# New written instruction orders for all five engines of a chunked-attention and attention-experts kernel

## The chip, the core and the metric

The kernel runs on one core of one Trainium2 chip. The metric is the device time of one execution in microseconds. The median of three runs of the kernel before is 377.94 us (377.81 to 377.98).

## What is computed

Eight batches of 576 rows. First an attention with 8 heads of 64 columns in which each chunk of 64 rows looks only at itself; its output, 512 columns wide, is the input x of a layer with four experts. Each expert is a causal attention over all 576 rows with a projection out; a softmax over the two largest gate logits of a row weighs the experts.

```python
scores = scale * np.matmul(q_c, k_c.transpose(0, 1, 2, 4, 3))     # per chunk of 64 rows
attn = np.exp(scores - max);  attn = attn / (sum + 1e-09)
x = np.matmul(attn, v_c)                                          # -> (B, S, H * D)
logits = x @ w_gate;  w = softmax over the 2 largest of 4
for e in range(E):
    q, k, v = x @ wq[e], x @ wk[e], x @ wv[e]
    a = softmax(where(causal, -1e9, scale * (q @ k.T)))
    out += mask_e * w_e * (a @ v @ wo[e])
```

## The kernel before

The kernel does not issue its instructions in the order in which its code runs. It builds a plan: `add` makes an `Op` for an engine with a closure that issues its instructions, the ops that it depends on, and the buffers it uses (2457 ops, the DMAs among them). `Plan.emit` then plays the plan on a clock of its own and calls the closures in turn. Each engine takes its ops strictly in the rank that the table `ORDER` (line 191) gives: a list of numbers for each of PE, DVE, ACT, Pool (GpSimd) and SP, where the number is the place of the op among the ops of its engine. The tables fix the order on each engine, and through the clock also which of the interchangeable buffers (8 banks of PSUM, 4 `at`, 2 `aT` and so on) an op gets. While the planner's clock is below `WARM` = 25 us and PE has nothing ready, it issues a warm-up matmul (line 847, 128x512 bf16, result not used).

The steps on PE, by the line of their matmuls:

- L471: scores of the chunked attention, quarters of the array (64x64), 32 matmuls for a group of 128 rows; most steps take two groups. L544: the same attention times v, also quarters, 32 matmuls a group. 36 groups in all.
- L369: transposes, 8 matmuls for a normalised tile `en` (first five groups), 14 for the weights `at` of one expert and batch.
- L589: projections of x to q and k, 12 matmuls of 256 or 320 columns in three passes (high and low parts). L443: v and the gate, 12 matmuls of 260 columns ("V"). L810: output projection, 6 matmuls of 512 columns ("output"). These use the full array.
- L686: expert scores, 6 or 12 matmuls with 64 rows of the array ("rows" form, as L369). L780: weights times v, 4 and 20 matmuls with 64 columns of the array ("cols" form).

`scores` (L686) needs two `at` buffers for its two experts and keeps them until their transposes are done. For a step of 128 or 256 columns, VectorE takes the minimum (L697), ScalarE the exponential (L709) and GpSimd the product with the gate (L731); L755 on ScalarE clears the banks that the transposes filled. In the chunked attention, L481 to L490 on VectorE, L486 on ScalarE and L499 on GpSimd (`en`) stand between L471 and the transposes; from the sixth group on the transposes are DMAs (L376, L385). The weights come in by DMA, and L415 (ScalarE) and L419 (VectorE or GpSimd) split them into high and low parts (`wvg_lo`, `wqk_lo`, `wo_lo`).

```python
for eng, text in ORDER.items():
    own = [o for o in self.ops if o.eng == eng]
    for r, k in enumerate(text.split()):
        own[int(k)].rank = r
...
    if got is None:
        if eng == "PE" and now < until:
            fill()
```

Of the kernel before, what the change touches and what calls it, by code (L numbers as in the profile page):

```python
# [186 lines left out]
def pool_t(n):  # L187
# [15 lines left out]
    """,  # L203
    "DVE": """
# [20 lines left out]
    """,  # L225
    "ACT": """
# [23 lines left out]
    """,  # L250
    "Pool": """
# [635 lines left out]
```

## Time and profile before

| | |
|---|---|
| median of 3 runs | 377.94 us |
| the profiled execution: device time | 378.73 us |
| its span, first to last instruction | 377.0 us |
| granted TensorE clock, mean | 0.998 |
| PE busy | 369.2 us, 98% of the span |
| weight loads (PEld) busy | 315.9 us |
| ScalarE, VectorE, GpSimd busy | 302.5, 265.9, 244.9 us |
| DMA | 57.25 MB, 152 GB/s |

The profile tells for each engine when an instruction started and how long it took, and for each hole which semaphore ended it. Matmuls are pipelined, and their ends are modelled: how long a step holds PE is read from the start of its first matmul to the start of the next step's. A matmul and its weight load are two instructions; the profile lists the loads as an engine of their own, PEld.

### The profile page before, as it was taken

The page shows a single profiled execution, that of the slowest core. Times are in us where ns is not written, and L with a number is a line of the kernel's source. Part 1 is how long each engine was busy: PE and PEld are TensorE (multiplying, and loading weights), DVE is VectorE, ACT ScalarE, POOL GpSimd, SP SyncE. Part 2 cuts the span into 40 slices and gives each one's busy share as a digit, 9 for nine tenths or more (in the row PEclk, how much of TensorE's full clock was granted, in tenths as well). Part 3 has the DMA queues.
Part 4 walks back from the last instruction along what each step waited for, and adds up shares of the span by engine and source line. Part 5 has one row for each costly group of instructions (what it writes and reads, how often), then busy time and mean ns, then how long its engine had stood idle before and what let it go on. Part 6 is the DMA issues. An engine that isn't in the chain of part 4 may idle for free.

```text
span 377.0 us, 13434 instructions
## 1 busy us (share of the span) xinstructions
PE 369.2 (98%) x5214; PEld 315.9 (84%) x5217; DVE 265.9 (71%) x895; ACT 302.5 (80%) x845; POOL 244.9 (65%) x447
## 2 busy tenths in 40 slices
PE   8999999999999999999999989999999999999996
PEld 3699889988889799887899789978898989976775
DVE  2778899679967953589697786867864675388631
ACT  2574799999987996898966889699985895799651
POOL 6481778996899059966774518998684039867700
PEclk9999999999999999999999999999999999999999
DMA  7968679579888703249799395669526002235634
GB/s 286 386 226 269 162 190 252 83 180 164 196 199 194 145 30 85 56 114 253 192 251 233 58 238 137 101 173 155 153 62 113 2 3 57 57 57 93 178 123 167
DMA packets 88624, 57.25 MB, mean 152 GB/s; under 512 B 68976, under 2 KB 69232, under 8 KB 88560
## 3 DMA queue, kind: packets, MB, share of 16 engines
q1 hardware_dynamic: 88416, 56.12, 59.0%
q8 instruction: 41, 0.67, 0.7%
q10 hardware_dynamic: 144, 0.26, 0.2%
q14 instruction: 23, 0.19, 0.2%
HBM read 30.42 MB, written 9.44 MB: 106 GB/s over the span
## 4 chain that ended last, share of the span: by engine, by line
PE 73%; ACT 10%; DMA 5%; DVE 4%; POOL 4%; issue 2%; SPq 1%; POOLq 0%; ACTq 0%; DVEq 0%
PE bank L589 19%; PE bank L810 14%; PE bank L443 11%; PE bank L780 11%; PE bank L686 8%; ACT at L709 5%; PE bank L544 4%; PE bank L369 4%; PE bank L471 3%; DMA wpT<-wp 2%; DMA vs<-in_vt_dram 1%; POOL at L731 1%; ACT et L385 1%; DMA qs<-in_qt_dram 1%; ACT e L486 1%
## 5 line engine op out<-in xcount | busy, mean ns | idle before, releaser
L731 POOL TENSOR_SCALAR at<-at,st,gate 128x192 f32<-128x192 f32 (+4 forms) x160 | 94.8, 604 | 12.2 <-DVE st L722 4.5
L709 ACT ACTIVATE at<-at,st 128x576 f32<-128x576 f32 (+4 forms) x160 | 89.7, 584 | 4.0 <-DVE st L697 3.8
L589 PE MATMUL bank<-xh,wqk_hi 128*128 128x256 f32 (+1 forms) x256 | 77.3, 302 | 0.0
L589 PE MATMUL bank<-xl,wqk_hi 128*128 128x256 f32 (+1 forms) x256 | 75.7, 296 | 0.0
L589 PE MATMUL bank<-xh,wqk_lo 128*128 128x256 f32 (+1 forms) x256 | 75.7, 296 | 0.0
L697 DVE CUSTOM_DVE_ANT_0 at<-bank,mask 128x320 f32<-128x320 f32 (+4 forms) x160 | 59.9, 421 | 13.7 <-PE bank L686 11.7
L499 POOL TENSOR_TENSOR en<-e,mx 128x512 f32<-128x512 f32 x36 | 37.5, 1054 | 29.1 <-DVE mx L490 25.1
L589 PEld LDWEIGHTS bank<-xh,wqk_hi 128*128 128x128 f32 x256 | 48.4, 189 | 2.3 <-issue 0.5
L589 PEld LDWEIGHTS bank<-xl,wqk_hi 128*128 128x128 f32 x256 | 48.5, 189 | 0.2
L589 PEld LDWEIGHTS bank<-xh,wqk_lo 128*128 128x128 f32 x256 | 48.5, 189 | 0.0
L780 PE MATMUL bank<-aT,vv 128*64 128x448 f32 (+4 forms) x384 | 46.9, 393 | 0.0
L780 PEld LDWEIGHTS bank<-aT,vv 128*64 128x64 f32 x384 | 24.6, 137 | 22.2 <-issue 15.5
L763 DVE STREAM_TRANSPOSE aT<-at 32x96 f32<-32x96 f32 x128 | 34.4, 269 | 11.8 <-PE bank L780 6.3
L385 ACT ACTIVATE et<-wpT 128x1024 uint16<-128x1024 uint16 x31 | 36.7, 1189 | 5.7 <-DMA wpT<-wp 5.4
L755 ACT ACTIVATE aT<-bank 128x128 f32<-128x128 f32 (+1 forms) x160 | 37.0, 338 | 3.3 <-PE bank L369 3.2
L385 ACT ACTIVATE aT<-wpT 128x1024 uint16<-128x1024 uint16 x32 | 38.2, 1199 | 1.0 <-DMA wpT<-wp 0.9
L443 PE MATMUL bank<-wvg_hi,xh 128*128 128x260 f32 x128 | 36.8, 288 | 0.0
L443 PE MATMUL bank<-wvg_lo,xh 128*128 128x260 f32 x128 | 36.2, 283 | 0.0
L443 PE MATMUL bank<-wvg_hi,xl 128*128 128x260 f32 x128 | 36.0, 281 | 0.0
L709 ACT ACTIVATION_READ_ACCUMULATOR at<-at,st 128x1 f32 (+1 forms) x160 | 35.4, 221 | 0.0
L376 POOL COPY wp<-at 128x1024 uint16<-128x1024 uint16 x32 | 32.6, 1034 | 0.2
L686 PE MATMUL bank<-kh,qh 64*128 64x288 f32 (+4 forms) x192 | 32.5, 325 | 0.2
(104 smaller groups left out, 896.8 us busy)
## 6 DMA issues: line engine op xcount, KB each, us to landing
ks<-in_kt_dram SPq DMA_DIRECT2D x36, 256.0 KB, 4.1
vs<-in_vt_dram SPq DMA_DIRECT2D x36, 256.0 KB, 4.4
qs<-in_qt_dram SPq DMA_DIRECT2D x35, 256.0 KB, 4.4
out_dram<-y SPq DMA_DIRECT2D x35, 256.0 KB, 2.1
at<-in_wqk_dram SPq DMA_DIRECT2D x4, 256.0 KB, 5.9
wpT<-wp SPq DMA_TRANSPOSE x63, 3.3
at<-in_wvg_dram SPq DMA_DIRECT2D x2, 260.0 KB, 4.8
at<-in_wo_dram SPq DMA_DIRECT2D x2, 256.0 KB, 6.5
```

Source lines behind the costliest of these rows:

```text
L385: act.activation(put().bitcast(U16).rearrange("p j (q x) -> p j q x", x=2), pt.t[:, :256 * n].rearrange("p (x j q) -> p j q x", x=2, j=n), ...
L443: pe.matmul(bk.t[0:rows, :W_VG], xp[:, k, cols], wp[:, k, :], start=(n == 0), stop=(n == 3 * KT - 1))
L499: pool.tensor_tensor(en.t.rearrange("p (s h k) -> p s h k", s=2, h=HP), ev, rv.to_broadcast([128, 2, HP, 64]), op=OP.mult)
L589: pe.matmul(bk.t[:, :c1 - c0], wp[:, k], xp[:, k, c0:c1], start=(n == 0), stop=(n == 3 * KT - 1))
L686: pe.matmul(bks[s].t[:rows(i), at:at + c1 - c0], q[own, cs], k[own, c0:c1], start=(x == 0), stop=(x == 2), skip_group_check=True)
L697: dve.tensor_tensor_reduce(out=a.t[:r, A_OFF[i] + c0:A_OFF[i] + c1], in0=bk.t[:r, at:at + w], in1=mask[:r, m0:m0 + w], scale=1.0, scalar=f ...
L709: act.activation(af, af, AF.Exp, scale=-1.0, bias=st.t[:r, 0, i, 0:1], accum_out=st.t[:r, 1, i, 0:1])
L731: pool.tensor_scalar(af, af, st.t[:r, 2, i, 0:1], gt.t[:r, i, e:e + 1], op0=OP.mult, op1=OP.mult)
L755: act.activation(dst, bk.t[:, s0:s0 + 64 * n].rearrange("p (j c) -> p j c", j=n), AF.Copy)
L763: dve.transpose(dst, src)
L780: pe.matmul(bk.t[64 * s:64 * s + 64, c0 - h0:h1 - h0], vs.t[:, j, 64 * (2 * pair + s):64 * (2 * pair + s) + 64], ts[s].t[:, 448 * j + c0:4 ...
L810: pe.matmul(bk.t[:, n0:n1], up[:, k, 128 * t:128 * t + 128], wp[:, k, n0:n1], start=(n == 0), stop=(n == 5), skip_group_check=True)
```

## The change

All five tables of `ORDER` are replaced. Nothing else is touched: the ops, their closures, buffers, costs and the planner are the same. Of the diff (the first lines of two tables; the other rows are numbers too):

```diff
 ORDER = {
     "PE": """
-3 0 9 4 1 6 2 5 57 61 12 10 7 55 63 53 13 8 11 16 14 58 64 18 60 62 59 73 15 75 76 20 74 56 54 17 68 66 67 65 90 24
+0 3 6 9 1 4 2 5 12 7 10 63 11 58 55 53 13 8 16 61 14 57 18 62 56 54 64 65 20 60 75 74 67 59 15 24 17 68 73 66 76 93
...
     "SP": """
-10 4 8 12 14 11 5 9 13 1 15 2 16 0 3 24 7 6 18 20 17 37 26 21 31 36 19 38 32 30 23 22 42 47 28 29 27 25 34 35 59 45
+8 4 10 9 12 14 0 1 15 3 11 5 16 13 2 24 7 6 20 18 17 37 26 21 31 38 36 19 30 32 22 23 42 47 28 29 59 27 25 45 35 33
```

PE holds 314 steps in both orders. Warm-up matmuls that the planner puts between them: 43 before, 51 now (10 and 5 ahead of the second step in both; then 17, 2, 2 and 7 before, and 15, 7, 4 and 10 now).

**The fifth batch's first groups on PE.** Before, in PE's row (L544 and L471 are the quarter steps; a row with another `et`, `vs`, `ks` or `qs` is another group):

```order
L544 MATMUL bank_65<-et_86,vs_80 64x64 x2
...
L544 MATMUL bank_65<-et_85,vs_77 64x64 x2
...
L544 MATMUL bank_63<-et_88,vs_78 64x64 x2
...
L544 MATMUL bank_63<-et_87,vs_79 64x64 x2
...
L471 MATMUL bank_68<-ks_75,qs_71 64x64 x2
...
L471 MATMUL bank_68<-ks_76,qs_72 64x64 x2
...
L686 MATMUL bank_62<-kh_102,qh_98 128x192
...
L471 MATMUL bank_61<-ks_73,qs_69 64x64 x2
...
L443 MATMUL bank_63<-wvg_hi,xch_89 128x260
```

The same groups' steps now:

```order
L544 MATMUL bank_61<-et_87,vs_80 64x64 x2
...
L544 MATMUL bank_61<-et_86,vs_78 64x64 x2
...
L471 MATMUL bank_68<-ks_73,qs_69 64x64 x2
...
L471 MATMUL bank_68<-ks_76,qs_72 64x64 x2
...
L810 MATMUL bank_62<-wo_hi,uh 128x512
...
L443 MATMUL bank_63<-wvg_hi,xch_89 128x260
...
L810 MATMUL bank_65<-wo_hi,uh 128x512
...
L471 MATMUL bank_64<-ks_74,qs_70 64x64 x2
...
L544 MATMUL bank_66<-et_85,vs_79 64x64 x2
...
L544 MATMUL bank_66<-et_88,vs_77 64x64 x2
...
L810 MATMUL bank_61<-wo_hi,uh 128x512
```

Seven groups' quarter work stood in one stretch with one score step in it; now four groups' stand together, then an output, a V and an output step, then three groups', then an output step.

**GpSimd while the weights come in.** Before, in GpSimd's row (`en` is the normalised tile of a group, which an L369 step on PE waits for):

```order
L499 TENSOR_TENSOR en_83<-e_81,mx_93 128x512
L499 TENSOR_TENSOR en_84<-e_82,mx_94 128x512
L419 TENSOR_TENSOR wqk_lo<-at_109,wqk_hi 128x512
L419 TENSOR_TENSOR wo_lo<-at_110,wo_hi 128x512
L499 TENSOR_TENSOR en_83<-e_81,mx_91 128x512
L419 TENSOR_TENSOR wo_lo<-at_110,wo_hi 128x512
L499 TENSOR_TENSOR en_84<-e_82,mx_92 128x512
```

Now:

```order
L499 TENSOR_TENSOR en_83<-e_81,mx_93 128x512
L419 TENSOR_TENSOR wqk_lo<-at_109,wqk_hi 128x512
L499 TENSOR_TENSOR en_84<-e_82,mx_94 128x512
L419 TENSOR_TENSOR wvg_lo<-at_107,wvg_hi 128x520
L499 TENSOR_TENSOR en_83<-e_81,mx_91 128x512
L419 TENSOR_TENSOR wo_lo<-at_110,wo_hi 128x512 x2
L499 TENSOR_TENSOR en_84<-e_82,mx_92 128x512
```

The fifth group's `en` (from `e_81`, `mx_91`) stood behind the first half of `wo_lo`; now it stands ahead of both halves, behind the second half of `wvg_lo`.

**The last batch's transposes on PE.** Before, two transposes of two experts' weights in a row, then the output step:

```order
L369 MATMUL bank_62<-ident,at_109 128x64 x2
L369 MATMUL bank_67<-ident,at_109 128x64 x2
...
L369 MATMUL bank_61<-ident,at_110 128x64 x2
L369 MATMUL bank_66<-ident,at_110 128x64 x2
...
L810 MATMUL bank_67<-wo_hi,uh 128x512
```

Now:

```order
L369 MATMUL bank_68<-ident,at_110 128x64 x2
L369 MATMUL bank_64<-ident,at_110 128x64 x2
...
L810 MATMUL bank_61<-wo_hi,uh 128x512
...
L369 MATMUL bank_63<-ident,at_109 128x64 x2
L369 MATMUL bank_64<-ident,at_109 128x64 x2
...
L810 MATMUL bank_68<-wo_hi,uh 128x512
```

An output step has come between the two, and the step behind them writes a bank that the first transpose filled.

## Rows read from the trace of the kernel before

**Rows 1.** The page's first part: busy time, share of the span and instructions of each engine.

```profile
PE 369.2 (98%) x5214; PEld 315.9 (84%) x5217; DVE 265.9 (71%) x895; ACT 302.5 (80%) x845; POOL 244.9 (65%) x447
```

**Rows 2.** The page's second part: TensorE's granted clock in 40 equal slices of the span, in tenths.

```profile
PEclk9999999999999999999999999999999999999999
```

**Rows 3.** The page's fourth part: the chain that ended last, its share of the span by engine.

```profile
PE 73%; ACT 10%; DMA 5%; DVE 4%; POOL 4%; issue 2%; SPq 1%; POOLq 0%; ACTq 0%; DVEq 0%
```

**Rows 4.** The waits of PE's matmuls over the whole span: who waited for whom, us in total, times, longest.

```profile
PE bank L471 <- issue: 1.3, 1, 1.3
...
PE bank L810 <- ACT aT L755: 0.6, 1, 0.6
```

**Rows 5.** PE in order of time from 216 to 223 us: start, length, instruction, count, and in brackets the idle time ahead of it and what ended it.

```profile
216.17 2.10 PE L544 MATMUL bank<-et,vs 64*64 64x64 f32 x128
218.09 1.11 PE L471 MATMUL bank<-ks,qs 64*64 64x64 f32 x64
...
220.11 0.33 PE L471 MATMUL bank<-ks,qs 64*64 64x64 f32 x2
221.76 0.69 PE L471 MATMUL bank<-ks,qs 64*64 64x64 f32 x30 [1.33 <-issue]
222.38 0.39 PE L443 MATMUL bank<-wvg_hi,xch 128*128 128x260 f32 x1
```

**Rows 6.** PE in order of time near the program's start, columns as in rows 5 (the profile has lost the record of one of the 17 warm-up matmuls from 8.63 us).

```profile
8.63 3.84 PE L847 MATMUL bank<-warm 128*128 128x512 bf16 x16
12.40 0.69 PE L471 MATMUL bank<-ks,qs 64*64 64x64 f32 x32
13.03 0.46 PE L369 MATMUL bank<-ident,en 64*128 64x64 f32 x8
...
17.95 0.47 PE L443 MATMUL bank<-wvg_hi,xh 128*128 128x260 f32 x1
```

**Rows 7.** The page's third part: one of the DMA queues, its packets, MB, and share of 16 engines' span.

```profile
q8 instruction: 41, 0.67, 0.7%
```

**Rows 8.** The DMA queues from 219.0 to 220.4 us alone, columns as in rows 7.

```profile
q1 hardware_dynamic: 226, 0.41, 83.4%
q8 instruction: 1, 0.02, 4.2%
```

**Rows 9.** Pieces of the chain that ended last, in order of time: start, length, engine and line, matmuls. Each is a whole step or a run of equal steps.

```profile
161.49 1.03 PE bank L369 x28
...
173.23 0.58 PE bank L369 x14
...
183.18 1.09 PE bank L471 x64
...
191.70 1.39 PE bank L810 x6
...
194.53 2.02 PE bank L471 x128
...
208.67 0.84 PE bank L686 x12
...
232.99 1.43 PE bank L589 x12
```

**Rows 10.** PE in order of time in two dense stretches, from 27 and from 192.9 us, columns as in rows 5.

```profile
27.24 0.46 PE L369 MATMUL bank<-ident,en 64*128 64x64 f32 x8 [0.30 <-POOL en L499]
27.63 1.16 PE L544 MATMUL bank<-et,vs 64*64 64x64 f32 x64
28.61 1.11 PE L471 MATMUL bank<-ks,qs 64*64 64x64 f32 x64
29.55 0.65 PE L544 MATMUL bank<-et,vs 64*64 64x64 f32 x32
...
192.93 0.28 PE L443 MATMUL bank<-wvg_hi,xh 128*128 128x260 f32 x1
...
194.46 2.10 PE L471 MATMUL bank<-ks,qs 64*64 64x64 f32 x128
196.48 0.39 PE L589 MATMUL bank<-xh,wqk_hi 128*128 128x256 f32 x1
...
198.02 0.31 PE L589 MATMUL bank<-xh,wqk_hi 128*128 128x320 f32 x1
```

**Rows 11.** GpSimd in order of time from 24 us, columns as in rows 5.

```profile
24.88 1.30 POOL L419 TENSOR_TENSOR wo_lo<-at,wo_hi 128x512 fp32r<-128x512 f32 x1 [1.52 <-ACT wo_hi L415]
26.15 1.04 POOL L499 TENSOR_TENSOR en<-e,mx 128x512 f32<-128x512 f32 x1
```

**Rows 12.** PE in order of time: the first row of a step and of the step behind it, at three places, columns as in rows 5.

```profile
86.05 1.61 PE L544 MATMUL bank<-et,vs 64*64 64x64 f32 x64
87.59 0.40 PE L686 MATMUL bank<-kh,qh 64*128 64x288 f32 x2
...
120.90 0.75 PE L686 MATMUL bank<-kh,qh 64*128 64x192 f32 x2
...
122.25 1.19 PE L544 MATMUL bank<-et,vs 64*64 64x64 f32 x64
...
344.74 1.10 PE L369 MATMUL bank<-ident,at 64*128 64x64 f32 x28
346.45 0.50 PE L810 MATMUL bank<-wo_hi,uh 128*128 128x512 f32 x1 [0.61 <-ACT aT L755]
```

134 rows, old and new, of the table ORDER are left out of this document.

## The prediction

> **What bounds the kernel now.** The page's first part comes first: TensorE is busy for 369.2 of 377.0 us, the next engine, ScalarE, for 302.5 [rows 1]. A busy PE need not be PE at its best, so the slices come next: its clock is granted in full in all forty [rows 2], and the time is not lost there. The chain that ended last runs over PE for 73% of the span [rows 3]. So what counts is how the steps on PE follow each other, and the wait view filtered to PE names the two largest holes behind the first microseconds: 1.3 us once at L471 for "issue", and 0.6 us at L810 for ScalarE [rows 4]. "Issue" means that PE waited for nothing that the profile shows: no semaphore ended that wait.
>
> PE in order of time shows the place. From 216.17 us it runs 128 quarter matmuls of L544, 64 of L471, 12 score matmuls and 2 of the next L471 step, then stands still until 221.76 [rows 5] (the score step's place is told in the order). The whole L471 step of one group lasts from 220.11 to 222.38, 2.27 us; the same step between other steps lasts from 12.40 to 13.03, 0.63 us [rows 6]. **The pause costs 1.64 us.**
>
> What came late? PE's matmuls and weight loads are 10,431 instructions [rows 1]; one DMA queue of kind "instruction" moved 41 packets, 0.67 MB [rows 7], one for every 254 of them. One of these packets lies inside 219.0 to 220.4 us, the stretch just ahead of the pause, in which the data queue took 83.4% of the DMA engines [rows 8]. I read the pause as PE waiting for its next block of instructions. From 216.17 to 220.11 it had run 204 matmuls, each with its own weight load: 408 instructions in 3.94 us, more than one packet holds. Where full steps run, one matmul and its load go every 0.12 us, so a packet feeds 15 us; a quarter step of 64 matmuls uses 128 instructions in about 1 us.
>
> [...]
>
> **Term 1: the pause goes, -1.64 us.** In the new order the five groups' steps that stood as L544, L544, L471, scores, L471 stand as L544, L471 (256 instructions), then output, V and output, then L471 and L544 (192 instructions). The three full steps between are 24 matmuls and last over 4 us at the rows of such steps (1.43 for twelve V or projection matmuls, 1.39 for an output step [rows 9]). From the stretch in which the late packet moved (219.0 to 220.4 [rows 8]) to the moment PE went on (221.76) it is under 2.8 us, so 4 us should be enough. Dense stretches remain elsewhere: the densest in the new order is L544, L544, L471 for five groups, 160 matmuls or 320 instructions in a row, and a pair of two-group L544 steps, 256, in two places. For these the rows speak: 168 matmuls from 27.24 to 30.20 us (29.55 + 0.65), 336 instructions in 2.96 us, ran with no hole behind the first wait, and 256 instructions from 194.46 to 196.48 ran with none either [rows 10]. So I take no new pause; the other end is one more of the same size.
>
> **Term 2: eight more warm-up matmuls, +1.78 us.** The planner fills PE's empty time up to 25 us of its own clock with L847 matmuls. The old order held 43, the new one 51. They are in PE's program and run even when the next step is ready. Seventeen of them last from 8.63 to 12.40 us, 0.222 each [rows 6]; eight cost 1.78. In front of the last of them both orders have done the same real work (four L471 steps, two transposes, two L544 steps), so all 306 steps that remain start that much later. Against this nothing can hide: PE has no idle time behind it into which 1.78 us would fit, except the waits of term 4. The lower end is 0, if in the old order the last matmuls had been waiting for data and the new order starts with data ready.
>
> **Term 3: changes of form, +0.57 us.** PE's steps have four forms (full, quarters, rows, cols), and a step costs more beside another form. A pair of two-group L471 steps lasts 2.02, one alone 1.09: a run of quarters costs 2 x 1.09 - 2.02 = 0.16. Two transposes together last 1.03, one alone 0.58: a run of rows costs 0.13 [rows 9]. A V step before quarters lasts from 192.93 to 194.46, 1.53, and a 256-column projection behind them from 196.48 to 198.02, 1.54 [rows 10], where twelve matmuls between full steps take 1.43 [rows 9]: a run of full steps costs 0.10 + 0.11, some 0.20. After the warm-up both orders have 306 steps and 16 runs of cols; full runs go from 32 to 36, quarter runs from 23 to 24, rows runs from 34 to 31. That is 4 x 0.20 + 0.16 - 3 x 0.13 = +0.57. Bounds: 0.13 to 0.20 for each of the two more runs, 0.3 to 0.8.
>
> **Term 4: other waits, -0.98 us.** Four are worth naming. (a) At 27.24 us the L369 step waits 0.30 us for the GpSimd product en [rows 10], which GpSimd began at 26.15, behind 1.30 us of wo_lo [rows 11]. In the new order this product stands ahead of both wo_lo pieces on GpSimd: gone. (b) At 344.74 two transposes last until the output step at 346.45, 1.71 us where a pair takes 1.03 [rows 9, 12]: 0.68 us, of which the profile shows 0.61 as PE waiting for ScalarE to clear the bank (aT, L755). In the new order an output step stands between the two transposes and gives ScalarE 1.4 us: gone. (c) The L544 step at 86.05 lasts until the score step at 87.59, 1.54 us, where a quarter step alone takes 1.09 [rows 9, 12]: 0.45. (d) Twelve score matmuls last from 120.90 to 122.25, 1.35 us, where twelve take 0.84 [rows 9, 12]; less 0.10 for the change of form (above, 0.16 to 0.20 for the two changes of a run), 0.41 is a wait. For these two I see no reason in the order that they go, nor that they grow, since every engine's order is new; I take them unchanged (0.86 us), with 0 and double as the ends.
>
> **What is moved beside PE.** All lists are new, so DMA issues on SP and the waits behind them shift too. Where GpSimd, VectorE and ScalarE are earlier or later by some us the time does not change as long as PE finds its inputs: they are busy 64 to 80% [rows 1]. The tail behind the last matmul is the same halves of the last output step, and I cost it at nothing.
>
> **Sum.** -1.64 + 1.78 + 0.57 - 0.98 = -0.27 us. The profiled execution took 378.73 us, its span 377.0 and 1.7 around it; it lies 0.8 above the median of the three runs, 377.94, and I carry the difference over to the median: **377.7 us**, no change that can be told (0.2% is 0.76 us, about what a measurement of this kernel can tell from none).
>
> **Rivals.**
> 1. *The pause moves instead of going* (slower). For it: the rows show that density alone does not decide, since 336 instructions in 2.96 us ran through and 408 in 3.94 us did not; where a packet ends and how busy the DMA engines are (83% ahead of the pause) must count too. The new order keeps 320 instructions in a row at one place, and a two-group pair right behind score steps and ahead of a values step. It decides once a packet's worth is used up before the next has come, some 4 us after the last. Against: only one of 41 did so before. Price: one pause, 377.7 + 1.64 = 379.3.
> 2. *The change doesn't do what it says.* If code is always in time, the pause belongs to something else in that stretch (the loads that began at 218 us, say) and stays: also 377.7 + 1.64 = 379.3. The packet in that stretch and the lack of any releaser speak against it.
> 3. *The waits shrink more than I take.* An order written anew may serve all four: -1.84 instead of -0.98, so 377.7 - 0.86 = 376.8, and 376.5 with term 3 at its lower end. For it: two of four go visibly. Against: score steps still follow score steps, and they need a new weight buffer each time.
> 4. *A new wait of that kind* of 0.5 to 1.3 us: 378.2 to 379.0.
>
> **How the numbers follow.** Forecast 0.46; rival 1 0.18, rival 2 0.05, rival 3 0.26, rival 4 0.05. The forecast's own spread (terms 2 and 3 down to their lower ends against the two waits doubled) leaves it mostly within 0.2%. Rival 3 makes the chance of faster 0.27 with a little of the forecast's lower side, rivals 1, 2 and 4 that of slower 0.27; the rest, 0.46, is no change. The range reaches from rival 3's lower time to rivals 1 and 2: 376.5 to 379.3.
>
> **What would show it.** Right: no "issue" wait of over 0.5 us on PE behind the warm-up; 51 warm-up matmuls, the first step behind them near 19.7 us instead of 17.95; the L369 step near 28 us without a wait for en; no wait of the output step for aT near the end; 1.0 to 2.0 us left in waits between. Wrong: an "issue" wait on a quarter step or right behind one (rival 1 or 2), or a first real step as early as before (term 2). If the time is below 377 with all steps as counted, it is rival 3.

## The result, and the profile after

The changed kernel took 381.96 us (median of 4 runs, 380.70 to 384.23), the kernel before 377.96 (4 runs, 377.81 to 378.34): ratio 1.0099, 95% interval 1.0075 to 1.0123. It is 4.0 us slower, where I had forecast 377.7 and no change that can be told. The range, 376.5 to 379.3, missed it too. These runs lie 3.5 us apart, those of the kernel before 0.5; but over the 18 to 23 runs of the kernel before that stand beside most experiments it is 2.2 to 3.0 us, so the small figure is one of few runs.

The profiled execution is the slowest of the four, 384.23 us. The page's first part and the chain by engine:

```profile
PE 373.2 (98%) x5221; PEld 318.2 (83%) x5225; DVE 266.6 (70%) x895; ACT 301.4 (79%) x845; POOL 245.0 (64%) x447
...
PE 60%; ACT 13%; POOL 9%; DMA 7%; DVE 6%; issue 4%; POOLq 0%; DVEq 0%; ACTq 0%
```

Beside [rows 1] PE's share tells nothing: it is busy for the same 98% (4.0 us more of a longer span, eight warm-ups among them). Beside [rows 3] the chain left PE for the other engines (73% to 60%), and "issue" doubled. PE's waits, in us in total, times, longest:

```profile
PE bank L544 <- issue: 1.6, 2, 1.4
PE bank L847 <- DVE warm L319: 1.2, 1, 1.2
PE bank L544 <- ACT et L385: 0.8, 1, 0.8
PE bank L589 <- issue: 0.6, 1, 0.6
PE bank L686 <- ACT aT L751: 0.5, 1, 0.5
PE bank L810 <- DVE st L697: 0.4, 1, 0.4
```

The two waits of [rows 4] are gone. In their place stand three "issue" waits at other lines and new waits for ScalarE and VectorE. PE in order of time shows the first two of the "issue" waits:

```profile
16.32 0.80 PE L544 MATMUL bank<-et,vs 64*64 64x64 f32 x36
17.32 0.68 PE L544 MATMUL bank<-et,vs 64*64 64x64 f32 x28 [0.21 <-issue]
17.93 2.33 PE L847 MATMUL bank<-warm 128*128 128x512 bf16 x9
20.20 0.69 PE L471 MATMUL bank<-ks,qs 64*64 64x64 f32 x32
20.82 0.71 PE L369 MATMUL bank<-ident,en 64*128 64x64 f32 x16
21.46 0.39 PE L589 MATMUL bank<-xh,wqk_hi 128*128 128x256 f32 x1
...
23.08 0.68 PE L544 MATMUL bank<-et,vs 64*64 64x64 f32 x28
25.20 0.33 PE L544 MATMUL bank<-et,vs 64*64 64x64 f32 x4 [1.44 <-issue]
```

Count what PE ran between the two holes: 28 + 9 + 32 + 16 + 12 (the whole L589 step) + 28 = 125 matmuls, 250 instructions with their loads, one packet of code (by the page 10,446 instructions and 41 packets, one for every 255). But these 250 took from 17.32 to 23.8 us. **This stretch is not dense: 39 instructions a microsecond**, where the 408 ahead of the pause before took 3.94 us [rows 5]. So the pause has not moved to another dense place. The DMA queues (queue: packets, MB, share of 16 engines) from 17.3 to 22.7 us, then from 22.7 to 23.8:

```profile
q1 hardware_dynamic: 1140, 2.08, 103.3%
...
q1 hardware_dynamic: 211, 0.38, 97.8%
q8 instruction: 1, 0.02, 5.8%
```

The weights and the first groups fill the DMA engines (103.3%, then 97.8%). At 17.32 us PE entered one block of code; the packet with the next starts to move only at 22.72, 5.4 us later, and PE goes on 2.48 us after it started. Nearly the same time lies between packet and matmul at 220 us before (by the trace 219.38 and 221.76, [rows 5, 8]), and at the third hole (177.53 and 180.01). **What is late here is the packet, and I read the load on the DMA engines as what makes it late**; how much lateness PE can bear depends on how long one block lasts it, here 6.5 us against the 7.88 that the next one took to come. Two runs below bear on this: b_load on the load, b_shift114 on the density.

To sum up an execution I took, for each of the 305 steps behind the warm-up, its time less the usual time of such a step (kind of step and changes of form, fitted to the steps before). The kinds add up to 323.3 us in both orders, the changes of form to 27.0 and 27.6. What a step takes beyond that is counted as a hole or a wait, so that the columns add up to PE's end by construction; what they tell is where the time lies. In us:

| execution | time | first step behind the warm-up | holes of code behind it | other waits |
|---|---|---|---|---|
| before | 378.73 | 17.95 | 1.65 | 2.8 |
| changed | 384.23 | 20.20 | 2.5 | 4.5 |
| changed, again (a_same) | 381.10 | 19.82 | 0.3 | 3.9 |
| a_shift48 | 379.37 | 18.93 | 0 | 3.4 |
| a48_qh | 377.97 | 19.49 | 0 | 1.4 |

For the changed kernel: 2.25 + 0.64 + 2.55 = 5.44 of the 5.50 us by which its execution is longer. In a_same, 0.8 below its own median, the holes give next to nothing; there the loss is the late start and the other waits.

### The profile page after: what moved, and what is told of

The parts are those of the page before. It is cut to its first block, busy times and chain, and to the rows that moved or that the text cites. A ratio compares the mean times of both kernels' runs of the same rounds, so it can differ in the third digit from the quotient of the medians.

```text
span 382.5 us, 13434 instructions
## 1 busy us (share of the span) xinstructions
PE 373.2 (98%) x5221; PEld 318.2 (83%) x5225; DVE 266.6 (70%) x895; ACT 301.4 (79%) x845; POOL 245.0 (64%) x447
## 4 chain that ended last, share of the span: by engine, by line
PE 60%; ACT 13%; POOL 9%; DMA 7%; DVE 6%; issue 4%; POOLq 0%; DVEq 0%; ACTq 0%
PE bank L589 15%; PE bank L810 10%; PE bank L780 8%; PE bank L443 8%; DMA wpT<-wp 7%; PE bank L686 6%; ACT at L709 6%; PE bank L847 4%; POOL at L731 3%; PE bank L369 3%; PE bank L544 3%; PE bank L471 3%; ACT et L385 3%; POOL wp L376 3%; POOL en L499 2%
## 5 line engine op out<-in xcount | busy, mean ns | idle before, releaser
L731 POOL TENSOR_SCALAR at<-at,st,gate 64x64 f32<-64x64 f32 (+4 forms) x160 | 95.3, 609 | 12.3 <-DVE st L722 7.9
L709 ACT ACTIVATE at<-at,st 128x448 f32<-128x448 f32 (+4 forms) x160 | 89.2, 570 | 3.8 <-DVE st L697 3.7
L589 PE MATMUL bank<-xh,wqk_hi 128*128 128x320 f32 (+1 forms) x256 | 77.3, 302 | 0.1
L589 PE MATMUL bank<-xh,wqk_lo 128*128 128x320 f32 (+1 forms) x256 | 75.6, 295 | 0.6 <-issue 0.6
L589 PE MATMUL bank<-xl,wqk_hi 128*128 128x320 f32 (+1 forms) x256 | 75.7, 296 | 0.0
L697 DVE CUSTOM_DVE_ANT_0 at<-bank,mask 128x192 f32<-128x192 f32 (+4 forms) x160 | 59.8, 422 | 5.5 <-PE bank L686 4.9
L589 PEld LDWEIGHTS bank<-xh,wqk_hi 128*128 128x128 f32 x256 | 48.4, 189 | 2.6 <-issue 1.5
L589 PEld LDWEIGHTS bank<-xl,wqk_hi 128*128 128x128 f32 x256 | 48.4, 189 | 0.3
L589 PEld LDWEIGHTS bank<-xh,wqk_lo 128*128 128x128 f32 x256 | 48.4, 189 | 0.0
L385 ACT ACTIVATE et<-wpT 128x1024 uint16<-128x1024 uint16 x31 | 36.8, 1189 | 10.5 <-DMA wpT<-wp 10.3
L780 PEld LDWEIGHTS bank<-aT,vv 128*64 128x64 f32 x384 | 25.2, 137 | 22.0 <-issue 14.6
L385 ACT ACTIVATE aT<-wpT 128x1024 uint16<-128x1024 uint16 x32 | 37.8, 1196 | 3.8 <-DMA wpT<-wp 3.8
L376 POOL COPY wp<-en 128x1024 uint16<-128x1024 uint16 x31 | 31.9, 1038 | 5.6 <-DMA wpT<-wp 5.2
L686 PE MATMUL bank<-kh,qh 64*128 64x288 f32 (+4 forms) x192 | 32.9, 326 | 0.6 <-ACT aT L751 0.5
```

The costliest lines, as they stand in the source:

```text
L376: pool.tensor_copy(p.t[:, :256 * n].rearrange("p (x n) -> p x n", x=2), src().bitcast(U16).rearrange("p (n x) -> p x n", x=2))
L385: act.activation(put().bitcast(U16).rearrange("p j (q x) -> p j q x", x=2), pt.t[:, :256 * n].rearrange("p (x j q) -> p j q x", x=2, j=n), ...
L589: pe.matmul(bk.t[:, :c1 - c0], wp[:, k], xp[:, k, c0:c1], start=(n == 0), stop=(n == 3 * KT - 1))
L686: pe.matmul(bks[s].t[:rows(i), at:at + c1 - c0], q[own, cs], k[own, c0:c1], start=(x == 0), stop=(x == 2), skip_group_check=True)
L697: dve.tensor_tensor_reduce(out=a.t[:r, A_OFF[i] + c0:A_OFF[i] + c1], in0=bk.t[:r, at:at + w], in1=mask[:r, m0:m0 + w], scale=1.0, scalar=f ...
L709: act.activation(af, af, AF.Exp, scale=-1.0, bias=st.t[:r, 0, i, 0:1], accum_out=st.t[:r, 1, i, 0:1])
```

## The experiments

Theory A: PE waits for code packets that the busy DMA engines bring late; where the blocks end in the work decides which of them hurt. Theory B: the time lies in waits for other engines that the order fixes. Theory C: it lies in the eight warm-up matmuls. Each but b_load, of which there is one execution, ran 4 to 12 times; the kernel before, beside them, took 378.0 to 378.2 us in the median.

**The changed kernel again (a_same).** No edit.

> The changed kernel once more, unaltered. Theory A (PE waits for late blocks of its code, and how late depends on the DMA engines): 381 to 383 us, a spread over 1 us between runs, and again 'issue' holes on PE near 24 us (1.44 in the first profile) and 179 us (0.56), of another length than before. Theory B (waits for other engines, fixed by the order): 382 within 0.5 us, the same waits with the same lengths (0.85 us at L544 near 271 us, 0.46 at L686 near 88 us).

381.91 us (380.52 to 383.49), ratio 1.0099 (1.0074 to 1.0124). The profiled execution, at 381.10, has no hole at 24 or 179 us. The DMA queues from 17.0 to 19.7 us and from 19.7 to 20.9, and PE behind them:

```profile
q1 hardware_dynamic: 550, 1.00, 102.2%
...
q1 hardware_dynamic: 250, 0.46, 101.1%
q8 instruction: 1, 0.02, 5.7%
```

```profile
22.72 0.69 PE L544 MATMUL bank<-et,vs 64*64 64x64 f32 x32
```

Same program, same place, a packet that starts at 19.75 us, 2.75 after PE has entered the block ahead of it (17.0, by the count of instructions) instead of 5.4: no hole, the step runs in one piece. The spread that A foresaw is there, 3.0 us, but 18 runs of the kernel before, beside these six, spread as far (377.69 to 380.70), so it tells little. And the waits that B named come back too, one as long (0.5 at L686 for aT), one shorter (0.4 at L544 for et, where it was 0.8); this execution without large holes is still 2.4 us above that of before, hole and all. Neither theory has it alone.

**Blocks shifted by 48 instructions (a_shift48), and a control (a_shift258).** Of the tables nothing changes; some warm-up matmuls are cut into pieces.

```diff
-    plan.emit(lambda: banks and pe.matmul(banks[-1], warm[:, 0:128], warm, start=True, stop=True), WARM)
+    done = []
+
+    def fill():
+        n = 2 if len(done) < 24 else 1          # control: 4, 43
+        done.append(n)
+        for _ in range(n):
+            banks and pe.matmul(banks[-1][:, 0:512 // n], warm[:, 0:128], warm[:, 0:512 // n], start=True, stop=True)
+    plan.emit(fill, WARM)
```

> The changed order, with the first 24 warm-up matmuls cut into two halves each: the same PE time, 48 more instructions, so every later step starts 48 instructions further on in its 256-instruction blocks. Theory A: the ends of the blocks no longer lie in the quarter steps at 24 and 179 us; the 'issue' holes there (2.2 us together with the one of 0.21 at 17 us) shrink to under 0.6, and the time is 1 to 2 us below the changed kernel's. Theory B: the same time as the changed kernel within 0.5 us.

> A control for a_shift48: the changed order with the first 43 warm-up matmuls cut into four quarters each, 258 more PE instructions, so that the steps lie in their 256-instruction blocks almost where they lie in the changed kernel (2 instructions off), while the warm-up is cut up even more. Theory A (the place of the block ends decides): 380.7 to 381.9 us and a spread over 1.5 us, as the changed kernel, less what a shorter warm-up gives (at most 0.9). If cutting the warm-ups is itself what gained 2.4 us in a_shift48, 379.6 or less.

a_shift48 took 379.53 us (378.37 to 382.10), ratio 1.0039 (1.0018 to 1.0061): 2.4 us less than a_same beside it, with no "issue" wait in its profile. Not all of it is the shift: its first step came 0.9 us earlier (18.93 us), which I had not expected, and a wait of 1.1 us near 56 us took as much back. The 0.9 us lie ahead of 8 us, half of them in a quarter step that took 0.69 us (at 5.27) and in a_same 1.13 (at 5.62). That step varies between executions with the same start too (1.13 in before, 0.69 in b_late), so this part need not come from the edit. The control went to 382.84 (381.98 to 383.36), above what I expected of it, with new holes:

```profile
13.56 1.40 PE L853 MATMUL bank<-warm 128*128 128x128 bf16 x22 [0.87 <-issue]
...
19.37 0.57 PE L544 MATMUL bank<-et,vs 64*64 64x64 f32 x23 [1.36 <-issue]
```

Cutting up the warm-ups is not what gains; with 258 instructions more in the first microseconds PE waits for "issue" twice, 0.87 and 1.36 us, which I read as running out of code (in the changed kernel the DMA share is 1.02 to 1.04 from 12 to 20 us). That the holes follow the place of the block ends the control does not show: at 24 and 179 us it has none, as a_same has none. B alone, which foresees the same time for all three, falls.

**The order before, blocks shifted by 114 (b_shift114).** The same edit with 4 pieces for the first 19 warm-ups.

> The order before on every engine; only the first 19 warm-up matmuls are cut into four quarters each, which puts 114 more PE instructions ahead of the work. Theory A (late code blocks): the block ends move 114 instructions back in the work; from the trace of before, with a block asked for some 2.0 to 2.8 us before its packet starts and usable 2.4 us after that, the holes grow from one near 220 us to several (near 57 us 2.1 to 2.9 us, near 218 us 2.0 to 2.8, near 300 us 0.4 to 1.2): 380.3 to 383. Theory B (waits for other engines only): 378.2 within 0.6, since no step changes its place.

381.30 us (379.67 to 383.72), ratio 1.0089 (1.0060 to 1.0117): **3.2 us from the place of the block ends, with every table as before.** Two holes in the profile, at 57 and 224 us; the one that I foresaw near 300 us did not come. What follows the first I had not foreseen. PE in order of time, and then the busy time by stretch (length, PE, PEld, DVE, ACT, POOL, granted clock, DMA share, GB/s):

```profile
55.74 1.03 PE L544 MATMUL bank<-et,vs 64*64 64x64 f32 x57
58.54 0.34 PE L544 MATMUL bank<-et,vs 64*64 64x64 f32 x7 [1.77 <-issue]
58.82 0.42 PE L589 MATMUL bank<-xh,wqk_hi 128*128 128x320 f32 x1
```

```profile
58.80:60.00 1.20, 1.20 (x12) 1.19 (x6) 0.43 (x1) 1.06 (x3) 1.05 (x4) 0.63 1.05 248
60.00:62.00 2.00, 2.00 (x10) 2.00 (x9) 1.72 (x7) 2.00 (x8) 0.32 (x1) 0.50 1.01 369
62.00:64.00 2.00, 2.00 (x14) 2.00 (x14) 1.47 (x6) 0.82 (x3) 1.89 (x3) 0.87 1.04 392
```

Behind the hole the granted clock falls to 0.50 for some 3 us (a matmul takes 0.47 us from 59.3 to 62.2, 0.31 in the same step before), and the steps of those microseconds take 1.5 us more than usual (3.84 us from the first matmul of L589 to the 16th, 2.30 before): a hole of 2.0 us cost 3.5.

The second hole is of another kind than those of the changed kernel. PE in order of time, and the DMA queues from 221.0 to 222.5 us:

```profile
221.28 2.10 PE L544 MATMUL bank<-et,vs 64*64 64x64 f32 x128
223.19 0.52 PE L471 MATMUL bank<-ks,qs 64*64 64x64 f32 x22
224.87 0.85 PE L471 MATMUL bank<-ks,qs 64*64 64x64 f32 x42 [1.15 <-issue]
```

```profile
q8 instruction: 1, 0.02, 4.9%
```

Nothing but the packet moves there. By the count of instructions PE entered the block before the packet's at 221.62; the packet started at 222.36, 0.74 us later, and PE went on 2.5 us after that. It waited all the same, because these quarter matmuls had used up the block in 1.9 us. **So there are two ways to such a hole: a late packet, as in the changed kernel, or work so dense that a packet in time is not soon enough.** That the holes are ends of blocks the count shows: with the semaphore waits of PE's sequencer counted in, all nine "issue" holes of over 0.2 us in the profiles (before, changed, b_load, a_shift258 and this one) end at an instruction whose number, divided by 256, leaves 189 to 193 (190 before; 191, 189 and 189 in the changed kernel; 193 twice in this one).

**One transfer more (b_load).** The order before, and a 2 MB copy between DRAM tensors at a place where nothing else moves.

```diff
+    o = plan.ops[2088]
+    def loaded(fn=o.fn):
+        nc.scalar.dma_start(scratch, qt[0:8])
+        fn()
+    o.fn = loaded
```

> The kernel before, with one more transfer of 2 MB from DRAM to DRAM (a copy of inputs that nobody reads), issued by ScalarE near 297.8 us, where the DMA engines are idle. On PE a quarter step of 128 matmuls runs there. In the profile of before the code packet of this place starts at 300.25 us, 1.2 us after PE's first instructions of the step before the block, and nothing else moves. Theory A (a packet is late because the DMA engines are busy): it starts 3 to 6 us later, near 303 to 306 us. If the packet has its own time, whatever the load, 300.0 to 300.6.

One execution, 378.40 us. The queues of before from 300.2 to 301.3 us, and of b_load from 297.4 to 302.2 and from 302.2 to 303.2:

```profile
q8 instruction: 1, 0.02, 5.8%
```

```profile
q10 hardware_dynamic: 18, 1.18, 62.9%
...
q8 instruction: 1, 0.02, 5.7%
q10 hardware_dynamic: 15, 0.00, 0.8%
```

The packet, at 300.25 us before, starts at 302.28, about when the first of the copy's last sixteen packets ends (64 KB each, starting from 299.7 us on, 2.7 us each). Since this execution runs 0.4 us ahead of that of before, the copy has held it up by some 2.4 us, less than the 3 to 6 I expected. No hole follows: the steps behind have few instructions, 22 and 19 matmuls from 302 to 304 and from 304 to 306 us, against 128 from 298 to 300. That load delayed this packet is shown; how much it does, the DMA share alone does not tell: at 103.3% and 102.2% the packets of the changed kernel and of a_same started 5.4 and 2.75 us after PE had entered the block before. The pause near 220 us is there as before, 1.42 us idle where [rows 5] have 1.33:

```profile
221.35 0.69 PE L471 MATMUL bank<-ks,qs 64*64 64x64 f32 x30 [1.42 <-issue]
```

**The quarter run broken (b_late).** The order before with one PE step moved behind two full ones: term 1 by itself.

```diff
-... 205 41 39 44 203 46 37 225 216 ...
+... 205 41 39 203 46 37 225 44 216 ...
```

> The order before with one step of PE moved: the two-group L471 step of 218.09 us goes behind the V step and the projection, so that the quarter matmuls in a row are 128 + 12 + 32 instead of 128 + 64 + 12 + 32. Theory A: the 'issue' hole of 1.65 us near 220 us is gone (under 0.3 left), two more changes of form cost 0.2: 376.4 to 376.9. Rival (the hole belongs to the loads of that stretch, not to the code): the hole stays, 378.2.

377.36 us (376.85 to 377.99), ratio 0.9977 (0.9967 to 0.9988). The hole is gone, and behind the warm-up nothing else differs by more than 0.2 us (the first step comes 0.45 us earlier, 17.50 against 17.95). In the profiled executions the waits fall by the 1.64 of term 1; in the medians the gain is 0.86, with 0.36 for changes of form on the other side. So the pause was real and curable, and by the medians worth about 1.2 us. Why that is less than 1.64 stays open: b_load, near the median of the kernel before, has a pause as long as that of the profile before.

**Eight warm-ups fewer (a_w43).** The changed order, the last 8 warm-ups left out.

```diff
+    left = [43]
+
+    def fill():
+        left[0] -= 1
+        if banks and left[0] >= 0:
+            pe.matmul(banks[-1], warm[:, 0:128], warm, start=True, stop=True)
+    plan.emit(fill, WARM)
```

> The changed order without its last 8 warm-up matmuls (43 as in the kernel before). Theory C (the eight warm-ups are what the change costs first, as predicted): 1.6 to 1.8 us below the changed kernel, since PE's steps behind them start that much earlier. Theory A: the block that PE waits for at 24 us starts to move at 22.7 us whenever PE asks for it, since the DMA engines are full until then; PE comes 1.75 us earlier and waits 1.75 us longer: the same time within 0.6 us, and an 'issue' hole of about 3 us near 22 us.

381.30 us (380.20 to 382.91), ratio 1.0088 (1.0064 to 1.0111): 0.6 us less than a_same, within the scatter of both, where 1.75 us of warm-ups are gone. PE where they stood:

```profile
18.86 0.46 PE L369 MATMUL bank<-ident,en 64*128 64x64 f32 x8
20.76 0.47 PE L369 MATMUL bank<-ident,en 64*128 64x64 f32 x8 [1.44 <-POOL en L499]
```

By these rows, more than by the medians, C falls, and so does the mechanism that A foresaw here: PE waits for GpSimd's product en, not for code. The warm-ups had filled a wait for data.

**The start of before, the rest of the change (start_before).** All five tables cut at the planner's 30 us: what before has issued by then stands first, in its order; the rest follows as in the change. PE's first row, against the change:

```diff
-0 3 6 9 1 4 2 5 12 7 10 63 11 58 ...
+3 0 9 4 1 6 2 5 57 61 12 10 7 55 ...
```

> The tables of before up to the planner's 30 us, those of the change for everything behind it. If the later start of the change (its first full steps 1.9 us later, behind GpSimd's first en) is what costs most, the loss there and the hole at 24 us go: 379 to 379.8. If the loss is in the waits of later stretches (85 to 121 us, 210 to 221 us), 381.5 to 382.

382.24 us (380.87 to 384.70), ratio 1.0126 (1.0092 to 1.0160). The first step is at 18.03 us again, and 1.8 us come back as waits near 40 and 54 us for results of VectorE and ScalarE (0.5 for xl, 0.3 for qh, 0.3 for kl). The late start alone is not what costs, or not in this order; since a cut through tables brings mismatches of its own, it settles no more.

**One op of ScalarE moved (a48_qh).** On top of a_shift48. In the changed order ScalarE's row has an et (L385) ahead of the qh that the score step near 118 us needs (120 us in the first profile of the changed kernel). ScalarE and then VectorE in that profile:

```profile
114.89 0.44 ACT L597 ACTIVATE qh<-bank 128x320 fp32r<-128x320 f32 x1
118.63 1.18 ACT L385 ACTIVATE et<-wpT 128x1024 uint16<-128x1024 uint16 x1 [3.30 <-DMA wpT<-wp]
119.71 0.42 ACT L597 ACTIVATE qh<-bank 128x320 fp32r<-128x320 f32 x1
```

```profile
120.16 0.49 DVE L602 SCALAR_TENSOR_TENSOR ql<-bank,qh 128x320 fp32r<-128x320 f32 x1 [3.24 <-ACT qh L597]
120.57 0.28 DVE L793 TENSOR_TENSOR ul<-bank,uh 128x128 fp32r<-128x128 f32 x1
120.88 2.26 DVE L763 STREAM_TRANSPOSE aT<-at 32x96 f32<-32x96 f32 x8
123.17 0.46 DVE L697 CUSTOM_DVE_ANT_0 at<-bank,mask 128x288 f32<-128x288 f32 x1
```

One late DMA transpose stops ScalarE for 3.30 us, behind it VectorE for 3.24, and PE twice: the score step waits for qh and ql (0.3 us at a weight load, for ql), and the output step 3 us later for the bank that L697 reads late (0.37).

```diff
 L597 ACTIVATE qh_98<-bank_61 128x320
-L385 ACTIVATE et_85<-wpT_117 128x1024
 L597 ACTIVATE qh_97<-bank_63 128x320
 L788 ACTIVATE uh<-bank_62 128x128
+L385 ACTIVATE et_85<-wpT_117 128x1024
```

> The changed order with the first 24 warm-up matmuls halved (as a_shift48, 379.53 us), and one op of ScalarE moved: et (L385), which waits 3.6 us for a DMA transpose at 113 us, goes behind qh (L597) and uh (L788). Nothing else moves on any engine. Theory W (the new waits of PE near 118 to 121 us, 0.57 + 0.54 us in every profile of the changed order, come from qh standing behind that et on ScalarE): the score step at 118 us and the output step at 122 us no longer wait, 378.3 to 378.7. If another engine is what ends those waits, 379.5 within 0.4.

378.37 us (377.16 to 380.27), ratio 1.0010 (0.9993 to 1.0027): 1.16 less than a_shift48, as expected. The runs of the two overlap (a_shift48 from 378.37 to 382.10), so the medians alone would not decide; the rows do. ScalarE, then PE, which no longer waits there:

```profile
114.74 0.44 ACT L597 ACTIVATE qh<-bank 128x320 fp32r<-128x320 f32 x1 [1.18 <-PE bank L589]
115.12 0.28 ACT L788 ACTIVATE uh<-bank 128x128 fp32r<-128x128 f32 x1
116.67 2.25 ACT L385 ACTIVATE et<-wpT 128x1024 uint16<-128x1024 uint16 x2 [1.27 <-DMA wpT<-wp]
```

```profile
118.39 0.38 PE L686 MATMUL bank<-kh,qh 64*128 64x288 f32 x2
...
120.83 0.39 PE L810 MATMUL bank<-wo_hi,uh 128*128 128x512 f32 x1
```

**A second one (a48_qh_clear).** On top of a48_qh, another et (L385) moved behind the bank clearings at 84 us; in ScalarE's table:

```diff
-... 221 54 169 182 185 184 183 181 186 193 ...
+... 221 169 182 185 184 183 181 186 54 193 ...
```

> As a48_qh, and a second op of ScalarE moved: the et (L385) ahead of the bank clearings at 84 us goes behind the first six of them (L751, L755), for the last of which the score step at 86 us waits 0.75 us. The planner then gives some later steps other banks. Theory W: that wait goes, 377.4 to 378.1. If it is the transposes on PE that end it, as a48_qh.

378.66 us (377.64 to 380.50), ratio 1.0013 (0.9995 to 1.0032): a miss, no change from a48_qh that can be told. The wait at 86 us shrinks from 0.76 to 0.49, and in the score step behind it 0.8 us now pass between two matmuls, for VectorE:

```profile
85.86 0.58 PE L686 MATMUL bank<-kh,qh 64*128 64x192 f32 x2 [0.27 <-ACT aT L751]
...
87.86 0.40 PE L686 MATMUL bank<-kh,qh 64*128 64x288 f32 x1 [0.39 <-DVE ul L793]
```

**Two joins (join275, join275_w36).** b_late up to the planner's 275 us, the changed tables behind it (cut as in start_before); then the same with `left = [36]` as in a_w43, without its last 7 warm-ups. The end of PE's table, against b_late:

```diff
-... 306 307 278 308 310 311 309 312 313
+... 307 306 278 310 311 309 308 312 313
```

> The order before with the L471 step moved (as in b_late) up to the planner's 275 us, the order of the change behind it, which has an output step between the two transposes near 345 us. The wait of 0.68 us for aT there goes, the earlier waits stay: 376.5 to 376.9. If the later stretch of the change has as many waits of its own, 377.2 to 377.5, as b_late.

> join275 without its last 7 warm-up matmuls, 1.5 us of PE ahead of the V step at 17.95 us. If a warm-up costs its own length (theory C), 1.3 to 1.5 us below join275. If PE then waits for x (the steps of VectorE, ScalarE and GpSimd between L544 and V) as it did for en in the run with 43 warm-ups, within 0.5 us of join275, with a wait of about 1.4 us ahead of the V step.

join275: 377.37 us (376.88 to 378.34), ratio 0.9985 (0.9972 to 0.9997), no better than b_late. The wait for aT near 345 us is gone and PE ends 0.65 us earlier, but the execution is as long: the last store landed 0.6 us later behind PE's end, and so it does in join275_w36 (the span ends 4.2 us behind PE in both, 3.5 in b_late); why stays open. join275_w36: 376.55 us (376.04 to 377.89), ratio 0.9960 (0.9946 to 0.9974), the fastest of all. Of the 1.5 us of warm-ups 0.8 came back, more than the 0.5 I allowed for a wait, less than C's 1.3; PE waits in two places instead, as in a_w43: 0.3 us in all at the start of the V step, and 0.3 in the projection behind it, for GpSimd's wqk_lo (L419).

## Why the prediction was wrong

The sum was right where it counted and wrong where it assumed: that no new pause comes, and that the other waits do not grow.

- **Term 1** (-1.64 us, no new pause): the pause went, as b_late shows for the same cause. What failed is the step "For these the rows speak", from which I took no new pause: I took density for the measure and looked for the densest run. Density is one half (b_shift114); the other is when the packet starts, 5.4 us after PE entered the block before in one execution of the changed kernel, 2.75 in another at the same place. So the holes came at 39 instructions a microsecond, behind the first loads, and near 179 us, where the DMA share ahead of the packet is 0.95 too. Rival 1 had the event and its condition right, a packet's worth used up before the next has come, but looked for it at dense steps; its some 4 us from one block to the next were 4.4 at the pause before, and 5.8, 7.9 and 5.7 at the holes of the changed kernel. 38 of the 41 packets of that execution passed without such a hole, as 40 did before. The rival's price of one pause was far below the 4.0. In medians 1.2 us went and, by a_shift48, up to 2.4 came, the earlier start of that run included.
- **Term 2** (+1.78 for eight warm-ups): the first step came 1.9 to 2.25 us later, the size I gave. That the size agreed is luck, since the mechanism was wrong. It was the lower end that I named and then set aside, with the difference that the order itself brings the wait: without the eight, PE waits 1.44 us for en.
- **Term 3** (+0.57): 0.64 by the fit above; no run has it by itself.
- **Term 4** (-0.98): both waits that I let go, at 27 and 345 us, are gone. What failed here is the step that took the other two unchanged, because I saw no reason in the order that they go or grow. The other waits grew by 1.1 us in a_same and by 1.7 in the first profile, where I had forecast 0.98 less; in a_same this is the largest part of the miss. The waits near 86 and 120 us, 0.9 together, are 2.2 in a_same (1.1 at 85 to 88 us, 1.1 at 118 to 121). For the second the reason stood in ScalarE's row, an op that waits for a DMA ahead of one that PE waits for, and I had not read that row: a48_qh removes it by moving one op. Rival 4 priced one such wait, at 0.5 to 1.3.
- That the profiled execution stands for the median: before, it was 0.8 above, and I carried the difference over. It does not lie in the pause, which is as long in b_load, at 378.40; the first step there comes 0.57 us earlier (17.38 against 17.95).

With the blocks shifted and one op of ScalarE moved, the changed order takes 378.37 us: two edits that leave PE's order as it is take away 3.5 of the 4.0 us, an earlier start included that need not be theirs. Open stays how much of the late start is kept to the end (a_w43 gave back 0.6 of 1.75, which the scatter covers, start_before nothing), and what the second wait, at 86 us, hangs on.

## What to carry to other kernels

Where a wait is put down to "issue", look at the instruction queue and the DMA share of that stretch: count PE's instructions from one hole to the next, and set two times against each other: how long PE takes for one packet's worth of instructions, and how long after its first one the next packet starts, with the time until PE goes on (2.4 to 2.5 us at five holes here). Either of them made holes here. Before reading an order for one engine, read the rows of the others for an op that waits on a DMA ahead of an op on whose result PE depends: here one late transfer that held ScalarE for 3.30 us was handed on to VectorE (3.24) and PE (0.37 at the output step). And take two profiles before pricing a pause: two executions of the changed kernel had 2.5 and 0.3 us of such holes.

## What was not expected of the hardware

- By the count of instructions, in the profiles of before and of the changed kernel, a code packet started at most 1.2 us after PE had entered the block before the packet's where the DMA share in between was under 0.3 (often ahead of that), and up to 3.6 and 5.4 us after where it was above 0.9. PE went on 2.4 to 2.5 us after the packet's start at their four holes and at the second of b_shift114, and in these two profiles it used no block sooner (2.38 and 2.44 us at the least).
- A hole of 2.0 us was followed by granted clocks of 0.63, 0.50 and 0.87 in the stretches from 58.8 to 64 us (b_shift114); the holes of 1.65 us before and of 1.76 in the changed kernel were not (1.00 behind both, from 221.8 to 224 and from 25.2 to 27 us). That execution has a mean granted clock of 0.996, and this stretch accounts for it by my estimate from those rows (1.2 x 0.37 + 2.0 x 0.50 + 2.0 x 0.13 = 1.7 of 382.0 us). In a_shift48 four of 11 executions have 0.993 to 0.996, in a48_qh four of 12 have 0.994 or 0.995, and they take 1.8 us more than the others (medians). None of them was profiled, so whether they hold such a stretch is not shown.
